# Attention and two feed-forward layers on one core: the product with v taken for two query tiles at once, and scores listed ahead of older work

## Chip, cores and metric

One core of a Trainium2 chip. The metric is the device time of one execution in microseconds (us). Engine names follow the profile: PE is TensorE (PEld its weight loads), DVE is VectorE, ACT is ScalarE, POOL is GpSimd, SP the queue that issues the DMAs.

## What is computed

Attention with a threshold, then two feed-forward layers on its output, all in float32:

```python
q, k, v: (4, 8, 576, 64)
scores = scale * q @ k.T
thresh = max(scores) - tau
scores = where(scores >= thresh, scores, -1e9)
attn = exp(scores - max(scores)); attn /= sum(attn) + 1e-9
x = (attn @ v) as (2304, 512)
h = x @ w_in1;  x = (h * sigmoid(1.702 h)) @ w_out1      # w_in (512, 2048)
h = x @ w_in2;  x = (h * tanh(softplus(h))) @ w_out2     # w_out (2048, 512)
```

## The kernel before

**Attention.** The 4 x 8 heads are worked in 16 pairs. A pair's 576 queries make four "full" tiles of 128 queries and one "mix" tile, in which the last 64 queries of both heads lie side by side; so there are 80 tiles, counted from 1 in this document. For each tile:

- `qk` (L600 is its matmul): the scores, both heads at once on the upper and lower 64 rows of PE's array, into the PSUM banks `sc`. A float32 matmul is two instructions in the profile; so a full tile's 4 matmuls are 8 instructions.
- `softmax_a`, once per head of the tile (144 times): DVE scales the scores into `ss` and takes their minimum (L622), POOL works out the threshold (L626), ACT takes the exponential into `p` (L629), DVE applies the threshold and sums (L632).
- `attend`: PE turns `p` by 128x128 transposes (L706, L701), ACT copies them from the banks `tb0` to `tb2` into `pm` and `pmt` (L717), PE multiplies with v (L731) into a quarter of the bank `tb3`, and ACT copies the result into `xo` (L738). The five chunks of keys of a full tile's product are 8 matmuls of 128 array rows by 64 columns (one per head and chunk, from `pm`) and 2 of 64 by 64 (from `pmt`), with 128 moving columns each.
- `scale_x`, once per pair: 1/sum goes through DRAM (`rt`, `r_d`, `rb`), POOL multiplies `xo` (L667) and a DMA stores it (L669).

**Weights.** A feed-forward weight arrives as float64 words. `conv_w` and `split_w` make of each 1/16 of a layer ("a weight" below) a high and a low part, by three passes on ACT (L380, L382, L400), one on POOL (L392) and four on DVE (L386, L389, L394, L402). From tile 41 on a new weight is started every 5 tiles, so 8 of the first layer's 16 weights are started inside attention. `val` goes through a ring of three buffers `sv`. The first `NWA` weights have memory of their own; those after them wait for `opened`, the end of all attention work, whose memory they take.

**Feed-forward layers.** `h1`/`o1` and `h2`/`o2`: 12 matmuls (24 for two halves) per step, L495, L540 and L911. Step h needs a weight and x; step o of a weight comes two steps later.

**Order.** Nothing is placed by hand. Every operation is listed with an engine, an estimated duration and a rank. `Order.run` plays the list through, gives each engine, whenever it is free, the ready operation of the lowest rank, and writes the program in that order; on the chip each engine then runs its own fixed sequence. A tile's scores have its number as rank, DVE's first pass 2.5 less (`SMR`), and `attend` runs two tiles behind (`AHEAD`) with the number of its own tile, products 0.1 less (`AR`). Where older transposes or products and newer scores are ready together, the older go first.

Of the kernel before, what the change touches and what calls it, by code (L numbers as in the profile page):

```python
# [21 lines left out]
DMA_RATE = 200e3  # L22
PR = 2
AR = 0.1
# [11 lines left out]
NSS = 4  # L36
NOUT = 2
NHS = 5
NWA = 12
# [161 lines left out]
def attention_then_two_ffn_kernel(  # L201
# [361 lines left out]
    nms = Ring(apool, "nm", 4, [128, 2], F32)  # L563
# [3 lines left out]
    pms = Ring(apool, "pm", NPM, [128, 512], F32)  # L567
    pmt = Ring(apool, "pmt", 2, [128, 128], F32)
# [106 lines left out]
    def attend(tl, ps, pair, rank):  # L675
# [3 lines left out]
        _, vr, _, kvr = head[b, hp]  # L679
        w = 128 if full else 64  # L680
        at = t * 128
        if t == 0:
            xo[b, hp] = xos.next()
        if full:
            plan = [(0, pms, (0, 1), 128, 512), (1, pms, (2, 3), 128, 512), (2, pmt, (4,), 128, 128)]
        else:
            plan = [(0, pms, (0, 1, 2, 3), 128, 512), (1, pmt, (4,), 64, 128)]
        where, copies, keys = {}, [], []
        for bank, ring, cs, rows, cols in plan:
            pn, kpn = ring.next()  # L690
            keys.append(kpn)
            for n, c in enumerate(cs):
                where[c] = (bank, n * 2 * w, pn)
            copies.append((bank, pn, kpn, rows, cols))

        def tr(cs):
            for c in cs:
                bank, c0, _ = where[c]
                if c == 4:
                    m = 64 * len(ps)  # L700
                    nc.tensor.transpose(tb[bank][0:m, 0:128], pair[:, 516:516 + m], ident)  # L701
                    yield
                    continue
                for i in range(len(ps)):
                    a = (P1 + 64 if i else 4) + c * 128
                    nc.tensor.transpose(  # L706
                        tb[bank][:, c0 + i * 128:c0 + (i + 1) * 128], pair[:, a:a + 128], ident)
                    yield

        for (bank, pn, kpn, rows, cols), (*_, cs, _, _) in zip(copies, plan):  # L710
            n = 1 if 4 in cs else len(ps) * len(cs)
            n = add("PE", n * 0.109 + (0.16 if bank == 0 else 0.0), lambda cs=cs: tr(cs),
                ps, [("tb", bank)], rank, steps=max(n, 2))
            if sch.fill is None and WARM:
                sch.fill = ("PE", n, 0.107, keep_warm)
            add("ACT", t_act(cols),
                lambda pn=pn, bank=bank, rows=rows, n=cols: nc.scalar.copy(pn[0:rows, 0:n], tb[bank][0:rows, 0:n]),  # L717
                [("tb", bank)], [kpn], rank)
        i = avn[0] % 2
        avn[0] += 1  # L720
        av, kav = tb[3][:, i * 128:i * 128 + w], ("tb", 3, i)

        def mm():
            for c in range(5):
                _, c0, pn = where[c]
                for i in range(2):
                    rows, at, vc = slice(0, 128), c0 + i * w, c * 128 + 64 * i
                    if c == 4:
                        rows = slice(64 * i, 64 * i + 64) if full else slice(0, 64)
                        at, vc = (0, 512) if full else (64 * i, 512 + 64 * i)  # L730
                    nc.tensor.matmul(  # L731
                        av[64 * i:64 * i + 64], vr[rows, vc:vc + 64], pn[rows, at:at + w],
# [3 lines left out]
        add("PE", len(CK) * 0.107 * (2 if full else 1) + 0.2, mm, keys + [kvr], [kav], rank - AR, steps=2 * len(CK))  # L736
        x, kx = xo[b, hp]
        add("ACT", t_act(w), lambda: nc.scalar.copy(x[:, at:at + w], av), [kav], [kx + (t,)], rank - AR)  # L738
        if not full:
            scaling.append(scale_x(b, hp))  # L740

    avn = [0]
# [32 lines left out]
    for gi, tl in enumerate(groups + [None] * AHEAD):  # L775
        first = len(sch.ops)
        if tl:
# [3 lines left out]
            if t == 0:  # L781
# [4 lines left out]
                  for i, bank in enumerate(qk(tl, gi))]  # L786
            marks.append(len(sch.ops) - 1)
            behind.append((tl, ps, pair, gi))
        if gi >= AHEAD:
            attend(*behind.pop(0))  # L790
# [208 lines left out]
```

## Time and profile before

| | |
|---|---|
| median of 3 runs | 1096.7 us (1096.17 to 1097.32) |
| the profiled execution's own time | 1097.12 us |
| its span, first to last instruction | 1095.3 us |
| busy: PE, DVE, ACT, POOL | 99%, 63%, 59%, 18% of the span |
| mean granted PE clock | 0.998 of full |
| first score of tile 1, of tile 41, of tile 80 | 5.80, 149.9, 292.1 us |
| first step of o1 | 311.9 us |

The profiled execution lies 0.4 us above the median; 1.8 us of its time lie outside the span. The last two rows cut the span in four: attention's first half, its second half, what is left of attention after the last scores (three steps of h1 are run among it), and the rest of the feed-forward layers. A busy PE in this profile is not a PE at its peak, since the ends of matmuls are modelled: what a group of matmuls costs is read from its start to the start of what follows.

### The profile page before, as it was taken

The numbers are of one execution on the slowest core, as the hardware profiler recorded it, in microseconds if no ns is written. First come the engines' busy times: TensorE is split into PE (matmuls) and PEld (weight loads), VectorE is DVE, ScalarE is ACT, GpSimd is POOL, SyncE is SP. The second block draws the span as 40 slices with busy tenths as digits, with TensorE's granted clock in tenths as the row PEclk, the third lists the DMA queues.
The fourth block names the chain that finished last, engine by engine and source line by source line (L and its number), as shares of the span: only waits on it lengthen the run. The fifth ranks groups of instructions, "written<-read, shape, count | busy, mean of one in ns | idle before, by whom it ended". The sixth has DMA issues, their size and how long they took to land.

```text
span 1095.3 us, 17534 instructions
## 1 busy us (share of the span) xinstructions
PE 1084.9 (99%) x6708; PEld 877.5 (80%) x6708; DVE 692.8 (63%) x1354; ACT 651.2 (59%) x1065; POOL 196.4 (18%) x198
## 2 busy tenths in 40 slices
PE   9999999999999999999999999999999999999998
PEld 7767776777778899888888888888888888888887
DVE  7868899999978645545522444566464555554544
ACT  5767777888856445444422444496655655655665
POOL 2323344455534303303200000000000000000000
PEclk9999999999999999999999999999999999999999
DMA  2223333444244255545510222500010010010010
GB/s 90 82 76 125 92 118 127 146 128 149 95 161 140 94 202 173 199 148 184 181 58 1 97 96 96 173 1 1 29 39 1 10 39 1 1 40 1 1 40 19
DMA packets 49156, 94.53 MB, mean 86 GB/s; under 512 B 6320, under 2 KB 24240, under 8 KB 49072
## 3 DMA queue, kind: packets, MB, share of 16 engines
q1 hardware_dynamic: 49072, 93.42, 25.7%
q8 instruction: 52, 0.85, 0.3%
q14 instruction: 32, 0.26, 0.1%
HBM read 70.78 MB, written 22.62 MB: 85 GB/s over the span
## 4 chain that ended last, share of the span: by engine, by line
PE 97%; ACT 1%; DVE 1%; issue 0%; POOL 0%; POOLq 0%; DVEq 0%; ACTq 0%
PE h L495 36%; PE tb L540 18%; PE tb L911 18%; PE tb L731 9%; PE sc L600 8%; PE tb L706 7%; PE tb L701 1%; PE tb L506 0%; DVE p L632 0%; DVE ss L622 0%; ACT p L629 0%; POOL nm L626 0%; ACT pm L717 0%; ACT xo L738 0%; ACT sv L380 0%
## 5 line engine op out<-in xcount | busy, mean ns | idle before, releaser
L873 ACT ACTIVATE ms<-ms 128x512 f32<-128x512 f32 (+1 forms) x240 | 131.4, 584 | 133.5 <-DVE ms L858 132.5
L495 PE MATMUL h<-xa,wh 128*128 128x512 f32 x640 | 197.5, 390 | 0.0
L495 PE MATMUL h<-x,wh 128*128 128x512 f32 (+1 forms) x640 | 165.2, 346 | 0.0
L495 PEld LDWEIGHTS h<-xa,wh 128*128 128x128 f32 x640 | 119.7, 188 | 24.7 <-issue 0.2
L521 ACT ACTIVATE t<-h 128x512 f32<-128x512 f32 (+1 forms) x80 | 44.5, 557 | 155.3 <-PE h L495 154.7
L632 DVE SCALAR_TENSOR_TENSOR p<-ss,nm,p 128x577 f32<-128x577 f32 x144 | 130.0, 926 | 8.1 <-ACT p L629 6.4
L629 ACT ACTIVATE p<-ss,nm 128x576 f32<-128x576 f32 x144 | 111.5, 785 | 37.9 <-DVE ss L622 37.4
L524 DVE SCALAR_TENSOR_TENSOR h<-t,h 128x512 f32<-128x512 f32 (+1 forms) x80 | 51.3, 642 | 121.4 <-ACT t L521 121.2
L883 DVE TENSOR_TENSOR ms<-ms,hs 128x512 f32<-128x512 f32 (+1 forms) x80 | 50.2, 636 | 122.3 <-ACT ms L873 122.2
L622 DVE TENSOR_SCALAR_CACHE_REDUCE ss<-sc,nqsc 128x576 f32<-128x576 f32 x144 | 112.2, 812 | 21.1 <-PE sc L600 20.4
L495 PEld LDWEIGHTS h<-x,wh 128*128 128x128 f32 x640 | 112.7, 189 | 15.8
L495 PE MATMUL h<-xa,wl 128*128 128x512 f32 x320 | 124.5, 389 | 0.0
L626 POOL TENSOR_SCALAR nm<-nm,tau_p 128x1 f32<-128x1 f32 x144 | 88.0, 612 | 168.0 <-DVE ss L622 163.6
L540 PE MATMUL tb<-gh,wh 128*128 128x512 f32 (+1 forms) x320 | 117.8, 368 | 0.0
L540 PE MATMUL tb<-gl,wh 128*128 128x512 f32 (+1 forms) x320 | 117.7, 368 | 0.0
L540 PE MATMUL tb<-gh,wl 128*128 128x512 f32 (+1 forms) x320 | 117.7, 368 | 0.0
L392 POOL TENSOR_TENSOR sv<-sv,sr 128x1024 uint32<-128x1024 uint32 x32 | 83.4, 2608 | 175.7 <-DVE sv L389 104.8
L911 PE MATMUL tb<-wh,g2h 128*128 128x512 f32 x288 | 112.1, 389 | 0.0
L911 PE MATMUL tb<-wl,g2h 128*128 128x512 f32 x288 | 112.1, 389 | 0.0
L911 PE MATMUL tb<-wh,g2l 128*128 128x512 f32 x288 | 112.0, 389 | 0.0
L495 PE MATMUL h<-x,wl 128*128 128x512 f32 (+1 forms) x320 | 110.9, 347 | 0.0
L600 PE MATMUL sc<-kq 64*128 64x288 f32 (+3 forms) x672 | 105.0, 417 | 1.0 <-DVE ss L622 0.9
(59 smaller groups left out, 1756.0 us busy)
## 6 DMA issues: line engine op xcount, KB each, us to landing
sr<-in_w_in SPq DMA_DIRECT2D x32, 512.0 KB
sr<-in_w_out SPq DMA_DIRECT2D x32, 512.0 KB
kq<-in_kq SPq DMA_DIRECT2D x16, 576.0 KB
sv<-x_d SPq DMA_DIRECT2D x16, 512.0 KB
w_d<-sv SPq DMA_DIRECT2D x16, 512.0 KB
sv<-w_d SPq DMA_DIRECT2D x16, 512.0 KB
vr<-in_v SPq DMA_DIRECT2D x16, 320.0 KB
x_d<-xo SPq DMA_DIRECT2D x16, 288.0 KB
```

Of the source, the lines that this page charges most:

```text
L392: lambda: nc.gpsimd.tensor_tensor(bits, bits, word(0), ALU.add), keys, [kval], rank, port=True)
L495: nc.tensor.matmul(hb[dst][:, 0:n], a[:, c, :], x[:, lo, c, 0:n], start=(i == 0), stop=(i == 3 * KD - 1))
L540: nc.tensor.matmul(accs[e][0][:, 0:n], a[:, es], b()[:, 0:n], start=(f == 0 and i == 0), stop=(f == KF - 1 and i == 2), skip_group_check=True,
L600: nc.tensor.matmul(dst, q, kq2[rows, k0:k0 + n], start=True, stop=True)
L622: lambda: nc.vector.tensor_scalar(n3, s3, nqsc, None, ALU.mult, ALU.min, accum_out=nm[:, 0:1]),
L626: lambda: nc.gpsimd.tensor_scalar(nm[:, 1:2], nm[:, 0:1], tau_p, 0.0, ALU.add, ALU.add),
L629: lambda: nc.scalar.activation(p[:, at:at + S], ns[:, 4:4 + S], AF.Exp, bias=nm[:, 0:1], scale=-1.0),
L632: lambda: nc.vector.scalar_tensor_tensor(p[:, whole], ns[:, 3 + i:4 + S + i], nm[:, 1:2], p[:, whole], ALU.is_le, ALU.mult, accum_out=sums ...
L706: nc.tensor.transpose(tb[bank][:, c0 + i * 128:c0 + (i + 1) * 128], pair[:, a:a + 128], ident)
L731: nc.tensor.matmul(av[64 * i:64 * i + 64], vr[rows, vc:vc + 64], pn[rows, at:at + w], start=(c == 0), stop=(c == 4))
L873: nc.scalar.activation(m()[:, 0:n], m()[:, 0:n], fn, bias=bias)
L911: nc.tensor.matmul(accs[t][0], x[:, t * 128:(t + 1) * 128], w, start=(f == 0 and i == 0), stop=(f == KF - 1 and i == 2), skip_group_check= ...
```

## The change

`attend` is split into `turn` and `product`. `turn` transposes one tile as before, but the copies of two neighbouring full tiles go into the same `pm` and `pmt` buffers, which are twice as wide, 128 columns of each tile in turn; the copies' destination is thus in pieces of 128 columns. After every second full tile (and after each mix tile) `product` is listed: the same 10 matmuls as for one tile, now with 256 moving columns, into half of `tb3`, followed by one copy of 256 columns to `xo`. It is no longer one operation of the list but three (chunks 0-1, 2-3, 4), each of which needs only its own copies, so other PE work may come between them; a key "product" keeps all products in sequence. Scores are ranked 8 tiles (`SF`) lower, so they go before any older transposes and products. `ss` has 6 buffers for 4, `nm` 8 for 4, and to make room the weights with memory of their own fall from 12 to 9. What is computed is the same.

```diff
--- before.py
+++ after.py
@@ -20,6 +20,7 @@
 SMR = 2.5
 DMA_US = 2.0
 DMA_RATE = 200e3
+SF = 8
 PR = 2
 AR = 0.1
 NORM_P = 1.0
@@ -33,10 +34,10 @@
 SLACK = 0.0
 AHEAD = 2
 NP = 8
-NSS = 4
+NSS = 6
 NOUT = 2
 NHS = 5
-NWA = 12
+NWA = 9
 NPM = 4
 NKQ = 2
 NXO = 2
@@ -560,12 +561,12 @@
     vrs = Ring(apool, "vr", NKQ, [128, 5 * 128], F32)
     pps = Ring(apool, "p", NP // 2, [128, P1 + S + 1], F32)
     sss = Ring(apool, "ss", NSS, [128, S + 5], F32)
-    nms = Ring(apool, "nm", 4, [128, 2], F32)
+    nms = Ring(apool, "nm", 8, [128, 2], F32)
     sms = Ring(apool, "sm", 2, [128, 32], F32)
     rts = Ring(apool, "rt", 1, [128, 32], F32)
     rbs = Ring(apool, "rb", 1, [128, S], F32)
-    pms = Ring(apool, "pm", NPM, [128, 512], F32)
-    pmt = Ring(apool, "pmt", 2, [128, 128], F32)
+    pms = Ring(apool, "pm", NPM, [128, 1024], F32)
+    pmt = Ring(apool, "pmt", 2, [128, 256], F32)
     xos = Ring(apool, "xo", NXO, [128, S], F32)
     xo = {}
     sm = {}
@@ -672,73 +673,89 @@
 
         return [multiply, spread, invert]
 
-    def attend(tl, ps, pair, rank):
+    def turn(tl, ps, pair, rank):
 
         kind, b, hp, t = tl
         full = kind == "full"
-        _, vr, _, kvr = head[b, hp]
-        w = 128 if full else 64
-        at = t * 128
         if t == 0:
             xo[b, hp] = xos.next()
         if full:
-            plan = [(0, pms, (0, 1), 128, 512), (1, pms, (2, 3), 128, 512), (2, pmt, (4,), 128, 128)]
+            if t % 2 == 0:
+                turned[b, hp] = [pms.next(), pms.next(), pmt.next()]
+            plan = [(0, (0, 1), 128), (1, (2, 3), 128), (2, (4,), 128)]
         else:
-            plan = [(0, pms, (0, 1, 2, 3), 128, 512), (1, pmt, (4,), 64, 128)]
-        where, copies, keys = {}, [], []
-        for bank, ring, cs, rows, cols in plan:
-            pn, kpn = ring.next()
-            keys.append(kpn)
+            turned[b, hp] = [pms.next(), pmt.next()]
+            plan = [(0, (0, 1, 2, 3), 128), (1, (4,), 64)]
+
+        def tr(bank, cs):
             for n, c in enumerate(cs):
-                where[c] = (bank, n * 2 * w, pn)
-            copies.append((bank, pn, kpn, rows, cols))
-
-        def tr(cs):
-            for c in cs:
-                bank, c0, _ = where[c]
                 if c == 4:
                     m = 64 * len(ps)
                     nc.tensor.transpose(tb[bank][0:m, 0:128], pair[:, 516:516 + m], ident)
                     yield
                     continue
                 for i in range(len(ps)):
-                    a = (P1 + 64 if i else 4) + c * 128
-                    nc.tensor.transpose(
-                        tb[bank][:, c0 + i * 128:c0 + (i + 1) * 128], pair[:, a:a + 128], ident)
+                    a, c0 = (P1 + 64 if i else 4) + c * 128, (n * len(ps) + i) * 128
+                    nc.tensor.transpose(tb[bank][:, c0:c0 + 128], pair[:, a:a + 128], ident)
                     yield
 
-        for (bank, pn, kpn, rows, cols), (*_, cs, _, _) in zip(copies, plan):
+        for (bank, cs, rows), (pn, kpn) in zip(plan, turned[b, hp]):
             n = 1 if 4 in cs else len(ps) * len(cs)
-            n = add("PE", n * 0.109 + (0.16 if bank == 0 else 0.0), lambda cs=cs: tr(cs),
+            cols = 128 * n
+            n = add("PE", n * 0.109 + (0.16 if bank == 0 else 0.0), lambda bank=bank, cs=cs: tr(bank, cs),
                 ps, [("tb", bank)], rank, steps=max(n, 2))
             if sch.fill is None and WARM:
                 sch.fill = ("PE", n, 0.107, keep_warm)
-            add("ACT", t_act(cols),
-                lambda pn=pn, bank=bank, rows=rows, n=cols: nc.scalar.copy(pn[0:rows, 0:n], tb[bank][0:rows, 0:n]),
-                [("tb", bank)], [kpn], rank)
+            src = tb[bank][0:rows, 0:cols]
+            dst = pn[0:rows, 0:cols]
+            if full:
+                dst = pn[0:rows].rearrange("p (g q) -> p g q", q=256)[:, :, t % 2 * 128:t % 2 * 128 + 128]
+                src = src.rearrange("p (g q) -> p g q", q=128)
+            add("ACT", t_act(cols), lambda src=src, dst=dst: nc.scalar.copy(dst, src),
+                [("tb", bank)], [kpn + (t % 2,)], rank)
+        if not full or t % 2:
+            product(tl, rank)
+
+    def product(tl, rank):
+
+        kind, b, hp, t = tl
+        full = kind == "full"
+        _, vr, _, kvr = head[b, hp]
+        w = 256 if full else 64
+        at = t // 2 * 256
+        pn = [p for p, _ in turned[b, hp]]
+        parts = ((0, 1), (2, 3), (4,)) if full else ((0, 1, 2, 3), (4,))
         i = avn[0] % 2
         avn[0] += 1
-        av, kav = tb[3][:, i * 128:i * 128 + w], ("tb", 3, i)
-
-        def mm():
-            for c in range(5):
-                _, c0, pn = where[c]
+        av, kav = tb[3][:, i * 256:i * 256 + w], ("tb", 3, i)
+
+        def mm(cs):
+            for c in cs:
                 for i in range(2):
-                    rows, at, vc = slice(0, 128), c0 + i * w, c * 128 + 64 * i
-                    if c == 4:
-                        rows = slice(64 * i, 64 * i + 64) if full else slice(0, 64)
-                        at, vc = (0, 512) if full else (64 * i, 512 + 64 * i)
+                    rows, vc = slice(0, 128), c * 128 + 64 * i
+                    if c < 4 and full:
+                        p, a = pn[c // 2], (c % 2 * 2 + i) * 256
+                    elif c < 4:
+                        p, a = pn[0], c * 128 + i * 64
+                    elif full:
+                        rows, p, a, vc = slice(64 * i, 64 * i + 64), pn[2], 0, 512
+                    else:
+                        rows, p, a = slice(0, 64), pn[1], 64 * i
                     nc.tensor.matmul(
-                        av[64 * i:64 * i + 64], vr[rows, vc:vc + 64], pn[rows, at:at + w],
+                        av[64 * i:64 * i + 64], vr[rows, vc:vc + 64], p[rows, a:a + w],
                         start=(c == 0), stop=(c == 4))
                     yield
 
-        add("PE", len(CK) * 0.107 * (2 if full else 1) + 0.2, mm, keys + [kvr], [kav], rank - AR, steps=2 * len(CK))
+        for cs, (_, kp) in zip(parts, turned[b, hp]):
+            add("PE", len(cs) * (0.49 if full else 0.13) + 0.05, lambda cs=cs: mm(cs),
+                [kp + (h,) for h in range(2 if full else 1)] + [kvr], [kav, "product"], rank - AR, steps=2 * len(cs))
         x, kx = xo[b, hp]
-        add("ACT", t_act(w), lambda: nc.scalar.copy(x[:, at:at + w], av), [kav], [kx + (t,)], rank - AR)
+        add("ACT", t_act(w), lambda: nc.scalar.copy(x[:, at:at + w], av), [kav],
+            [kx + (j,) for j in ((t - 1, t) if full else (t,))], rank - AR)
         if not full:
             scaling.append(scale_x(b, hp))
 
+    turned = {}
     avn = [0]
     scaling = []
 
@@ -783,11 +800,11 @@
             sums, ksum = sm[b, hp]
             pair, kpair = pps.next()
             ps = [softmax_a(sums, ksum, 5 * i + t, gi, bank, (pair, kpair), i)
-                  for i, bank in enumerate(qk(tl, gi))]
+                  for i, bank in enumerate(qk(tl, gi - SF))]
             marks.append(len(sch.ops) - 1)
             behind.append((tl, ps, pair, gi))
         if gi >= AHEAD:
-            attend(*behind.pop(0))
+            turn(*behind.pop(0))
             for todo in list(scaling):
                 todo.pop()(gi - AR, [marks[min(gi, len(marks) - 1)]] if tl else [])
                 if not todo:
```

How this moves instructions is seen in the programs' order (L706, L701, L731 of before are L699, L694, L744 of the change; L600 and L400 are one line further down). `tb0` to `tb3`, `sc`, `p`, `pm` and `pmt` are the tiles named above, with buffer numbers; "x4" means four equal matmuls in a row.

First place, on PE: what stands ahead of the first scores of pair 4 (tile 16). Before, the last 11 of the 19 rows between the scores of tile 15 and these:

```order
L731 MATMUL tb3_94<-pm2_174,vr0_154 64x128 x4
L731 MATMUL tb3_94<-pm3_175,vr0_154 64x128 x4
L731 MATMUL tb3_94<-pmt0_176,vr0_154 64x128 x2
L701 MATMUL tb2_93<-ident_100,p1_157 128x128
L706 MATMUL tb0_91<-ident_100,p2_158 128x128 x4
L701 MATMUL tb1_92<-ident_100,p2_158 64x128
L731 MATMUL tb3_94<-pm0_172,vr0_154 64x128 x4
L731 MATMUL tb3_94<-pm1_173,vr0_154 64x128 x4
L731 MATMUL tb3_94<-pmt1_177,vr0_154 64x128 x2
L731 MATMUL tb3_94<-pm2_174,vr0_154 64x64 x8
L731 MATMUL tb3_94<-pmt0_176,vr0_154 64x64 x2
L600 MATMUL sc0_98<-kq1_153 128x288
```

And now, all rows between the same two scores, and what follows:

```order
L699 MATMUL tb1_92<-ident_100,p2_152 128x128 x4
L699 MATMUL tb0_91<-ident_100,p3_153 128x128 x4
L694 MATMUL tb2_93<-ident_100,p3_153 128x128
L699 MATMUL tb1_92<-ident_100,p3_153 128x128 x4
L601 MATMUL sc0_98<-kq1_147 128x288
L601 MATMUL sc1_99<-kq1_147 128x288
L601 MATMUL sc0_98<-kq1_147 128x288
L601 MATMUL sc1_99<-kq1_147 128x288
L744 MATMUL tb3_94<-pm2_174,vr0_148 64x256 x4
```

Before, everything left of the older tiles, four tiles' products among it, stood ahead of these scores; now four rows of transposes do, and a product's first parts follow the scores.

Second place, on PE: around the scores of tile 54, in pair 11. Before, what stands between the scores of tiles 54 and 55:

```order
L731 MATMUL tb3_94<-pm2_174,vr0_154 64x128 x4
L731 MATMUL tb3_94<-pm3_175,vr0_154 64x128 x4
L731 MATMUL tb3_94<-pmt0_176,vr0_154 64x128 x2
L706 MATMUL tb0_91<-ident_100,p3_159 128x128 x4
L706 MATMUL tb1_92<-ident_100,p3_159 128x128 x4
L701 MATMUL tb2_93<-ident_100,p3_159 128x128
L600 MATMUL sc0_98<-kq0_152 64x288
```

And now:

```order
L744 MATMUL tb3_94<-pm1_173,vr1_149 64x256 x4
L699 MATMUL tb1_92<-ident_100,p2_152 128x128 x4
L699 MATMUL tb0_91<-ident_100,p3_153 128x128 x4
L694 MATMUL tb2_93<-ident_100,p3_153 128x128
L601 MATMUL sc0_98<-kq0_146 128x288
L601 MATMUL sc1_99<-kq0_146 128x288
L601 MATMUL sc0_98<-kq0_146 128x288
L601 MATMUL sc1_99<-kq0_146 128x288
L744 MATMUL tb3_94<-pm2_174,vr1_149 64x256 x4
L744 MATMUL tb3_94<-pmt1_177,vr1_149 64x256 x2
L699 MATMUL tb1_92<-ident_100,p3_153 128x128 x4
L699 MATMUL tb0_91<-ident_100,p0_150 128x128 x4
```

A product was one piece of ten matmuls for one tile; now its three parts (pm1, pm2, pmt1) serve two tiles, and transposes and scores stand between the first part and the other two.

Third place, on ACT: the first layer's weights around the end of attention. `t` and `gh` are made by each step of h1 from its bank `h`, `wh` is the high part of a weight. Before, around weight 9 (weights are counted from 0):

```order
L526 CAST gh2_147<-h1_3114 128x512
L400 CAST wh9_134<-sv2_115 128x1024
L521 ACTIVATE t0_143<-h2_3115 128x512
L380 ACTIVATE sv1_114<-sr2_112 128x1024
L382 ACTIVATE sr2_112<-sr2_112 128x1024
L526 CAST gh0_145<-h2_3115 128x512
L521 ACTIVATE t1_144<-h3_3116 128x512
L400 CAST wh10_136<-sv0_113 128x1024
```

And now:

```order
L522 ACTIVATE t1_138<-h1_2736 128x512
L527 CAST gh2_141<-h1_2736 128x512
L401 CAST wh9_3055<-sv2_115 128x1024
L401 CAST wh10_3057<-sv0_113 128x1024
L401 CAST wh11_3059<-sv1_114 128x1024
L381 ACTIVATE sv2_115<-sr0_110 128x1024
L522 ACTIVATE t0_137<-h2_2737 128x512
```

The high parts of weights 9, 10 and 11 waited for nothing but their own data; now they stand in one piece, need the memory of attention, and the `t` of a later step stands behind them.

## Rows read from the trace of the kernel before

**Rows 1.** Windows: stretch, us, busy of PE, PEld, DVE, ACT, POOL, PE's clock, DMA.

```profile
149.90:292.10 142.20, 141.10 (x1426) 101.07 (x1425) 137.21 (x316) 117.52 (x237) 71.33 (x84) 1.00 0.42 137
5.80:149.90 144.10, 141.81 (x1407) 101.86 (x1406) 121.16 (x303) 101.17 (x216) 48.16 (x78) 0.99 0.28 86
```

**Rows 2.** The chain that ended last, in order of time: start, us, what.

```profile
311.94 2.94 PE tb L540 x12
314.88 2.72 PE h L495 x12
...
1080.55 10.92 PE tb L911 x48
```

**Rows 3.** Timeline of PE, 199 to 204: start, us, array rows*columns, shape, instructions.

```profile
199.69 1.09 PE L731 MATMUL tb<-pm,vr 128*64 128x128 f32 x16
200.71 0.44 PE L731 MATMUL tb<-pmt,vr 64*64 64x128 f32 x4
201.08 1.09 PE L706 MATMUL tb<-ident,p 128*128 128x128 f32 x8
...
202.21 1.20 PE L600 MATMUL sc<-kq 64*64 64x288 f32 x10
203.34 0.66 PE L706 MATMUL tb<-ident,p 128*128 128x128 f32 x4
```

**Rows 4.** Timeline of PE, 286 to 290; the first three are a mix tile's.

```profile
286.44 0.69 PE L731 MATMUL tb<-pm,vr 128*64 128x64 f32 x16 [0.33 <-ACT pm L717]
287.06 0.33 PE L731 MATMUL tb<-pmt,vr 64*64 64x64 f32 x4
287.32 1.09 PE L706 MATMUL tb<-ident,p 128*128 128x128 f32 x8
...
288.45 1.24 PE L600 MATMUL sc<-kq 64*128 64x288 f32 x8
289.62 1.09 PE L731 MATMUL tb<-pm,vr 128*64 128x128 f32 x16
```

**Rows 5.** Timeline, 62 to 67; in brackets the idle time before, and its end.

```profile
62.03 1.24 PE L600 MATMUL sc<-kq 64*128 64x288 f32 x8
63.30 0.82 DVE L622 TENSOR_SCALAR_CACHE_REDUCE ss<-sc,nqsc 128x576 f32<-128x576 f32 x1 [5.63 <-PE sc L600]
64.18 1.97 PE L600 MATMUL sc<-kq 64*128 64x288 f32 x8 [0.91 <-DVE ss L622]
66.85 1.51 PE L706 MATMUL tb<-ident,p 128*128 128x128 f32 x7 [0.44 <-DVE p L632]
```

**Rows 6.** Windows, the stretch behind it.

```profile
67.20:70.50 3.30, 3.30 (x15) 2.15 (x13) 1.90 (x6) 2.58 (x5) 1.20 (x2) 0.50 0.01 2
```

**Rows 7.** Groups by line and shape: busy us, mean ns of one, idle before.

```profile
L402 DVE TENSOR_TENSOR wl<-sv,wh 128x1024 fp32r<-128x1024 f32 x32 | 40.0, 1251 | 16.1 <-ACT wh L400 16.1
L394 DVE SCALAR_TENSOR_TENSOR sv<-sr,sv 128x1024 uint32<-128x1024 uint32 x32 | 38.8, 1216 | 9.5 <-POOL sv L392 9.4
L382 ACT ACTIVATE sr<-sr 128x1024 f32<-128x1024 uint32 x32 | 37.3, 1169 | 0.0
L400 ACT CAST wh<-sv 128x1024 fp32r<-128x1024 f32 x32 | 33.8, 1056 | 14.4 <-PE tb L540 8.4 <-DVE sv L394 5.9
L386 DVE TENSOR_SCALAR sv<-sv 128x1024 f32<-128x1024 f32 x32 | 28.1, 879 | 5.0 <-ACT sv L380 5.0
L389 DVE TENSOR_SCALAR sv<-sv 128x1024 uint32<-128x1024 uint32 x32 | 25.9, 809 | 0.3
```

**Rows 8.** Timeline of attention's end, 308 to 331.

```profile
309.14 0.66 PE L706 MATMUL tb<-ident,p 128*128 128x128 f32 x4 [0.73 <-DVE p L632]
310.99 0.69 PE L731 MATMUL tb<-pm,vr 128*64 128x64 f32 x16 [1.09 <-ACT pm L717]
...
330.08 0.59 ACT L526 CAST gh<-h 128x512 fp32r<-128x512 f32 x1
330.25 0.33 SPq L669 DMA_DIRECT2D x_d<-xo  x1
```

## The prediction

> **What bounds the kernel now.** I read the chain of waits first, in order of time. From 311.9 us on it is PE alone: 12 matmuls every 2.72 us to the last group at 1080.6 [rows 2]. Nothing in the diff touches these steps, so their 783 us stay, and the change can only move the moment at which the first step of o1 starts.
>
> Then windows over attention, cut where the scores of tile 41 and of tile 80 start. In both halves PE is busy nearly throughout, but DVE differs: 121.2 of 144.1 us in the first half, 137.2 of 142.2 in the second, where the weights are prepared beside attention [rows 1]. So the first half is PE's, and the second belongs to PE and DVE together.
>
> A busy PE says little here, so I read PE's timeline from start to start. A full tile's product takes 1.39 us (199.69 to 201.08), nine transposes 1.13 (to 202.21), a mix tile's scores 1.13 [rows 3]; a full tile's scores take 1.17 (288.45 to 289.62), a mix tile's product 0.88 (286.44 to 287.32) [rows 4]. The reader is to see one more thing there, the price of changing the array's shape (rows*columns in the timeline; I call a stretch of one shape a run). 16 instructions of 128 columns cost 1.02 us, 16 of 64 columns 0.62: 64 columns are worth 0.40, so 128 stream for 0.80 and 0.22 is the run's own. For the four 64*64 ones it is 0.37 against 0.26, so 0.15 is the run's own [rows 3, 4]. Transposes have a run of 0.16 if each takes 0.108.
>
> Last, where PE loses time. Ahead of pair 4's scores stand four tiles' older work. DVE runs dry for 5.63 us, then PE waits 0.91 and 0.44 for DVE [rows 5], and right behind it, from 67.2 to 70.5, the granted clock is 0.50, which is 1.2 GHz where the rest has 2.4 [rows 6].
>
> **The change, part by part.**
>
> *Wider products.* Half as many product instructions of twice the columns stream as long. What falls is runs. Counted over PE's order up to the last product: 345 changes of shape before, 290 now. In one piece each the wider products would save two runs per pair of tiles, 64; their cutting into parts gives some back, and other neighbours join. 55 x 0.16 = 8.8 us less PE work. The bounds: if a run costs more the longer its instructions are (the 8 of 288 columns: 1.17 less 0.91 of streaming at the above rate leaves 0.26), some 80 long product runs cost 0.1 each more than I count, and 1 us is left; at 0.22 for all it is 12.
>
> *Scores first.* The same counts, up to the first score of tile 41: 163 changes of shape before, 129 now; 314 transposes before, 288 now; products of 30 full and 7 mix tiles before, 28 and 6 now. A full product streams for 0.80 + 0.22 = 1.02 us, a mix one for half of it. So 34 x 0.16 = 5.4, 26 x 0.108 = 2.8, and 2 x 1.02 + 0.5 = 2.5 of streaming lie no longer ahead of these scores: 10.7 us. The crowding before pair 4 goes too (four rows of transposes are left there): its two waits, 1.35, and half of 3.3 us at half the clock, 1.65, make 3.0. First half: -13.7.
>
> In the second half PE's work falls by 26 runs, 7 transposes and one product: 4.2 + 0.8 + 1.0 = 6.0. But DVE must follow. Its order now has one weight more between these scores (7, 7, 6 and 5 of the four passes, for 6, 6, 5 and 4): 0.88 + 0.81 + 1.22 + 1.25 = 4.2 us [rows 7], and one L632 of 0.8 less. 137.2 + 4.2 - 0.8 = 140.6 of the 142.2 it had. Second half: -1.6, DVE full.
>
> What was put off comes after the last scores: 56 transposes for 23, products of 6 full and 2 mix tiles for 3 and 1, 18 changes of shape for 13: 3.6 + 3.6 + 0.8 = 8.0 us more PE work. The rest of attention took 19.8 us (292.1 to 311.9), with 0.73 and 1.09 of waits at its end [rows 8]. These go: DVE has five threshold passes and one weight left after the last scores, about 9 us, and PE some 24 us of other work before it needs the last of them. Rest: +6.2.
>
> Sum: -13.7 - 1.6 + 6.2 = -9.1.
>
> *Copies.* The copies to `pm` write four pieces of 128 columns. No row shows that form. From below it costs nothing; from above I take the nearest strided destination, L382 at 1169 ns against the plain L400 at 1056, 11% [rows 7]. Even if all of ACT's 117.5 us in the second half grew by 11%, 13 us, its 24.7 idle us cover it [rows 1]. I take zero. 32 fewer copies to `xo` come off an engine that isn't the bound: zero.
>
> *Buffers.* Two more `ss` and four more `nm` take no time. Fewer own weights: weights 9 to 11 wait for attention's memory, thus for the last store. It was issued 18.3 us after o1's start, 21.1 after the last threshold pass let PE go on (309.1 to 330.25) [rows 8]. Now the last threshold pass comes about 16 us ahead of o1's start (9 after the last scores, of 26), so the store is issued about 5 us after it. On ACT the high parts of weights 9 to 11 stand behind the `gh` of step 5, which ran 18.2 us after o1's start [rows 8]. Covered by 13 us: zero.
>
> *Queues.* The DMAs are the same. The loads of v wait for products that come later, and the next pair's k and q stand behind them on SP; five tiles of scores, some 17 us, lie between. Zero.
>
> **A rule against these numbers.** By rows, a matmul's fixed cost is at most 0.22/16 = 14 ns, if the whole of a run's own cost is put on its instructions; 640 fewer instructions then save 9.0 us, as the runs do [rows 4]. The Trainium skill, page "TensorEngine Tiling (Array Packing)", section on instruction overhead, gives each matmul about 60 cycles, and one column the latency of sixty. At 2.4 GHz that is 25 ns, an estimate from that page, and 640 instructions would save 16 us; the sum would be -16.3.
>
> **Rivals.**
>
> *PE alone is the bound* (0.22). If weights slide or DVE's passes wait less for POOL, the second half gains its 6.0 and some of what PE lost there. -13.7 - 6.0 + 6.2 = -13.5: 1083.6, down to 1080. For it: PE is busy 141.1 of 142.2 us there. Against: DVE is full too.
>
> *DVE swallows the head start* (0.14). Scores can be early only as far as DVE takes them from two `sc` tiles. If the first half wins its 10.7 without the waits, the second nothing, and the rest still pays 6.2, it is -4.5: 1092.6. For it: DVE 96% busy in the second half. Against: the first half has 23 us of idle DVE.
>
> *A cost per matmul, not per run* (0.04). At 25 ns each, 7.2 us more than the 8.8: 1080.8. Against: 16 half-length instructions take 0.62 us; streaming 0.40 and 16 x 25 ns make 0.80. The page named above gives this price.
>
> *The late weights stall* (0.04), the slower case. If the last store lands later than 23 us after o1's start, the three casts on ACT (3 us), `t`, `gh` and `gl` of step 6 and the three DVE passes behind them, some 9 us in all, no longer fit before o1's step 6, at 6 x 2 x 2.72 = 32.6; each us later costs one, so the whole is slower than before from 32 on, some 27 later than worked out. Landed at 37 it costs 14: 1102. Against: that needs a chain of 21 us to become more than twice as long.
>
> *Clock or order gone wrong* (0.04). Each stretch like that at 67.2 costs 1.65. It came after PE had waited; six of them eat the gain, and more make it slower: 1099.
>
> The forecast has 0.52.
>
> **How the numbers follow.** The profiled execution took 1097.1 us, 0.4 above the median. 1097.1 - 9.1 = 1088.0. The likeliest case alone reaches from 1085 to 1091. The range, 1080 to 1093.5, takes in PE alone and DVE's swallowing; what is left out is part of the two ends, under 2 in 10. A change under 0.2%, 2.2 us, can't be told from none here. Faster: 0.52 + 0.22 + 0.04 and most of 0.14, less a little for what I have not seen, 0.86; same 0.06; slower 0.08.
>
> **What would show it.** Right: the first score of tile 41 at about 136 us for 149.9, of tile 80 at about 277 for 292.1, o1's first step near 303 for 311.9, and steps of 2.72 us from there on. A two-tile product in one piece takes 2 x 1.02 of streaming and runs of 0.22 and 0.15 from start to start, 2.4 us against 2 x 1.39. No 5 us of idle DVE before pair 4, and no halved clock there. Wrong: score starts no earlier at tile 41 (the order's counts are not what PE is bound by); tile 80 as early as 272 (PE alone); waits of PE for `ss` in the second half over 8 us (DVE swallows); a gap in the steps after o1's start, ended by a cast of weights 9 to 11 (late weights).

## The result, and the profile after

The change made the kernel slower: 1112.7 us median (1109.5 to 1113.5, 4 runs) for 1096.97, a ratio of 1.0134 with an interval of 1.0121 to 1.0148. 1088.0 was forecast, so both the sign and the range were missed. The profiled execution took 1113.5 us, its span 1111.7.

First the windows that answer to [rows 1], cut where the scores of tile 41 and of tile 80 and the first step of o1 start, and two short stretches that answer to [rows 6]. The columns are start and end, length, then busy time of PE, PEld, DVE, ACT and POOL, the granted clock, DMA.

```profile
core 0: us, PE busy (x) PEld busy (x) DVE busy (x) ACT busy (x) POOL busy (x), PEclk, DMA share, GB/s
5.80:143.80 138.00, 133.31 (x1041) 83.37 (x1040) 115.46 (x297) 93.83 (x189) 40.99 (x77) 1.00 0.29 91
143.80:297.30 153.50, 141.22 (x1100) 87.85 (x1100) 141.31 (x317) 113.42 (x217) 69.25 (x84) 0.97 0.39 122
297.30:328.30 31.00, 25.69 (x203) 18.42 (x203) 25.62 (x38) 23.45 (x44) 11.24 (x7) 1.00 0.44 145
195.10:198.40 3.30, 3.30 (x17) 1.71 (x15) 2.50 (x8) 0.77 (x2) 1.02 (x2) 0.50 0.24 64
222.40:229.20 6.80, 6.50 (x40) 4.18 (x40) 4.66 (x11) 3.16 (x8) 1.01 (x2) 0.50 0.14 38
```

The first half took 138.0 us for 144.1, 6.1 less (13.7 was forecast). The second took 153.5 for 142.2, 11.3 more (1.6 less), and the rest of attention 31.0 for 19.8, 11.2 more (6.2). Here is the chain of waits where attention ends, beside [rows 2].

```profile
322.36 0.48 ACT pm L714
...
325.46 0.37 ACT xo L753
325.83 0.22 ACT sr L383
...
326.78 0.59 ACT pm L714
...
327.41 0.95 PE tb L744 x20
328.36 2.96 PE tb L541 x12
331.32 2.72 PE h L496 x12
```

From o1's first step on nothing changed: steps of 2.72 us, and 1111.7 - 328.3 = 783.4 us to the end, as before. The loss lies ahead of it, and the reader sees the new link of the chain: ACT's copy to `pm`, and the work ahead of that copy on ACT.

PE is no longer busy throughout: in the second half 12.3 of 153.5 us are idle, where [rows 1] had 1.1 of 142.2. What it waited for in attention, in us, times and the longest, first in the kernel before:

```profile
PE tb L706 <- DVE p L632: 1.5, 3, 0.7
PE tb L731 <- ACT pm L717: 1.4, 2, 1.1
PE tb L731 <- ACT xo L738: 1.1, 3, 0.4
PE sc L600 <- DVE ss L622: 0.9, 1, 0.9
```

and in the changed kernel:

```profile
PE tb L744 <- ACT pm L714: 10.1, 15, 1.7
PE sc L601 <- DVE ss L623: 7.2, 7, 2.2
PE tb L699 <- ACT pm L714: 1.7, 4, 0.6
PE tb L744 <- ACT xo L753: 1.4, 3, 0.5
```

4.9 us have become 20.4: products wait for their copies, and scores for DVE. With idle stretches too short for this list (under 0.15 us), PE was idle for 5.2 us of attention before and for 22.3 now, as the windows have it. Waits can also hide in time that the view counts as busy. Read from start to start, as the prediction reads costs, with all that a run of one shape takes beyond its own cost counted as a wait, the two traces give some 13 and 38 us, by an estimate from all of PE's runs; the 13 and 37 us named in the expectations below are to be read against these.

How a product comes to wait shows in two timelines of the changed kernel. Of PE (start, length, instruction, in brackets the idle time ahead and what ended it):

```profile
300.30 1.95 PE L744 MATMUL tb<-pm,vr 128*64 128x256 f32 x16 [0.58 <-ACT pm L714]
302.17 0.65 PE L744 MATMUL tb<-pmt,vr 64*64 64x256 f32 x4
302.75 0.66 PE L699 MATMUL tb<-ident,p 128*128 128x128 f32 x4
303.25 0.38 PE L694 MATMUL tb<-ident,p 128*64 128x128 f32 x2
305.31 0.69 PE L744 MATMUL tb<-pm,vr 128*64 128x64 f32 x16 [1.68 <-ACT pm L714]
...
322.89 1.95 PE L744 MATMUL tb<-pm,vr 128*64 128x256 f32 x16 [1.74 <-ACT pm L714]
...
327.41 0.69 PE L744 MATMUL tb<-pm,vr 128*64 128x64 f32 x16 [1.30 <-ACT pm L714]
```

and of ACT ahead of the wait of 1.68 us:

```profile
300.77 2.79 ACT L630 ACTIVATE p<-ss,nm 128x576 f32<-128x576 f32 x4
303.45 0.38 ACT L753 COPY xo<-tb 128x256 f32<-128x256 f32 x1
303.70 1.07 ACT L401 CAST wh<-sv 128x1024 fp32r<-128x1024 f32 x1
304.65 0.61 ACT L714 COPY pm<-tb 128x512 f32<-128x512 f32 x1
```

The four transposes of the mix tile that this product needs first are done at about 303.4. Their copy stands on ACT behind four exponentials, a copy to `xo` and a weight cast, and starts 1.2 us later, at 304.65; the product stands next in PE's queue, so PE waits 1.68 us.

### The profile page after: what moved, and what is told of

Read it like the earlier page. It is cut to its first block, busy times and chain, and to the rows that moved or that the text cites. A ratio compares the mean times of both kernels' runs of the same rounds, so it can differ in the third digit from the quotient of the medians.

```text
span 1111.7 us, 16158 instructions
## 1 busy us (share of the span) xinstructions
PE 1084.3 (98%) x6068; PEld 850.6 (77%) x6068; DVE 692.3 (62%) x1358; ACT 646.5 (58%) x1033; POOL 182.4 (16%) x198
## 4 chain that ended last, share of the span: by engine, by line
PE 90%; ACT 5%; DVE 3%; issue 1%; DMA 1%; SPq 0%; POOL 0%; DVEq 0%; ACTq 0%; POOLq 0%
PE h L496 35%; PE tb L541 18%; PE tb L928 18%; PE sc L601 7%; PE tb L744 7%; PE tb L699 4%; ACT pm L714 2%; ACT p L630 1%; DVE p L633 1%; DVE ss L623 1%; PE tb L694 0%; PE tb L507 0%; ACT pmt L714 0%; DMA vr<-in_v 0%; ACT sr L383 0%
## 5 line engine op out<-in xcount | busy, mean ns | idle before, releaser
L633 DVE SCALAR_TENSOR_TENSOR p<-ss,nm,p 128x577 f32<-128x577 f32 x144 | 134.2, 953 | 25.9 <-ACT p L630 13.2
L630 ACT ACTIVATE p<-ss,nm 128x576 f32<-128x576 f32 x144 | 108.7, 790 | 17.2 <-DVE ss L623 17.1
L601 PE MATMUL sc<-kq 64*128 64x288 f32 (+3 forms) x672 | 107.4, 421 | 7.3 <-DVE ss L623 7.2
L393 POOL TENSOR_TENSOR sv<-sv,sr 128x1024 uint32<-128x1024 uint32 x32 | 80.7, 2523 | 187.0 <-DVE sv L390 133.2
L627 POOL TENSOR_SCALAR nm<-nm,tau_p 128x1 f32<-128x1 f32 x144 | 76.9, 534 | 183.3 <-DVE ss L623 177.6
```

Of the source, the lines that this page charges most:

```text
L393: lambda: nc.gpsimd.tensor_tensor(bits, bits, word(0), ALU.add), keys, [kval], rank, port=True)
L601: nc.tensor.matmul(dst, q, kq2[rows, k0:k0 + n], start=True, stop=True)
L627: lambda: nc.gpsimd.tensor_scalar(nm[:, 1:2], nm[:, 0:1], tau_p, 0.0, ALU.add, ALU.add),
L630: lambda: nc.scalar.activation(p[:, at:at + S], ns[:, 4:4 + S], AF.Exp, bias=nm[:, 0:1], scale=-1.0),
L633: lambda: nc.vector.scalar_tensor_tensor(p[:, whole], ns[:, 3 + i:4 + S + i], nm[:, 1:2], p[:, whole], ALU.is_le, ALU.mult, accum_out=sums ...
```

## Experiments

Each table row is one kernel: its time, its ratio to the kernel before with the interval, then the idle time of PE just ahead of products, scores and transposes in attention by the trace's groups of instructions, and the changes of array shape up to the last product, counted as in the prediction.

| kernel | us | ratio | products | scores | transposes | changes |
|---|---|---|---|---|---|---|
| before | 1096.97 | 1 | 2.7 | 1.0 | 1.5 | 345 |
| changed | 1112.7 | 1.0134 [1.0121, 1.0148] | 12.0 | 7.3 | 3.0 | 290 |
| e1 wide product, old order | 1121.8 | 1.0227 [1.0206, 1.0247] | 7.0 | 17.1 | 2.6 | 269 |
| e2 scores first, old product | 1089.0 | 0.9932 [0.9917, 0.9947] | 0.2 | 1.4 | 0.8 | 359 |
| e3 buffers alone | 1095.9 | 0.9996 [0.9986, 1.0005] | 1.7 | 1.5 | 1.8 | 343 |
| e4 changed, SF = 2 | 1105.4 | 1.0072 [1.0053, 1.0091] | 9.5 | 5.5 | 1.8 | 286 |
| e5 paired, 128 columns | 1096.25 | 0.9997 [0.9988, 1.0007] | 0.0 | 4.1 | 3.6 | 312 |
| e6 changed, products put off | 1092.8 | 0.9959 [0.9947, 0.9971] | 0.5 | 5.4 | 1.5 | 274 |
| e7 products put off, SF = 4 | 1081.2 | 0.9859 [0.9842, 0.9876] | 0.5 | 2.9 | 0.3 | 265 |
| e8 changed, SF = 4 | 1094.9 | 0.9979 [0.9970, 0.9989] | 9.0 | 3.3 | 2.1 | 285 |
| e9 changed, five pairs of p | 1103.3 | 1.0065 [1.0050, 1.0080] | 9.7 | 3.3 | 2.8 | 299 |
| e10 changed, 4 ss | 1097.7 | 1.0012 [1.0002, 1.0021] | 5.2 | 1.4 | 7.1 | 273 |
| e11 changed, no GpSimd pass | 1100.6 | 1.0037 [1.0023, 1.0052] | 10.8 | 1.7 | 2.9 | 290 |
| e12 e7, product in one piece | 1092.9 | 0.9972 [0.9959, 0.9985] | 2.1 | 3.4 | 4.4 | 243 |
| e13 e8, no GpSimd pass | 1090.9 | 0.9950 [0.9935, 0.9964] | 8.8 | 2.6 | 1.4 | 285 |
| e14 e7, 128 columns | 1091.3 | 0.9953 [0.9938, 0.9968] | 0.5 | 0.9 | 2.2 | 324 |
| e15 e6, 4 ss | 1088.4 | 0.9925 [0.9911, 0.9940] | 0.5 | 3.2 | 2.0 | 270 |
| e16 e7, 4 ss | 1082.2 | 0.9872 [0.9855, 0.9888] | 0.9 | 2.8 | 0.7 | 267 |

**Which part of the change it is.** e1 is the wide product alone:

```diff
-SF = 8
+SF = 0
```

> The widened product alone: scores keep the rank of their own tile (SF = 0), all else as in the changed kernel. PE's order up to the last product has 269 changes of array shape, for 345 before and 290 with the whole change. Theory A (putting the scores first is what makes PE wait): the waits of PE in attention fall back to the 13 us of before, and 76 x 0.16 = 12 us of work are gone: about 1084.5 us. Theory B (the widened product makes PE wait, since it needs the copies of two tiles and leaves less other work between a copy and its use): the 37 us of waits stay, and 1112.7 less 21 x 0.16 is about 1109 us.

e2 is the scores first alone, e3 the buffers alone, both on the kernel before; e4 is the changed kernel with `SF = 2`.

```diff
+SF = 4
-NSS = 4
+NSS = 6
-NWA = 12
+NWA = 9
-    nms = Ring(apool, "nm", 4, [128, 2], F32)
+    nms = Ring(apool, "nm", 8, [128, 2], F32)
-                  for i, bank in enumerate(qk(tl, gi))]
+                  for i, bank in enumerate(qk(tl, gi - SF))]
```

> The scores first alone, with the product of one tile at 128 columns as before, and the change's buffers (6 ss, 8 nm, 9 own weights). The scores are ranked 4 tiles ahead, not 8: PE's order is then the same row for row as with 8. 359 changes of shape for 345: 2.2 us more work. Theory A: the waits of PE come as in the changed kernel, 37 for 13 us: about 1097 + 2 + 24 = 1123 us. Theory B: the waits stay near 13 us: 1097 to 1101 us.

> The kernel before with the change's buffers alone: 6 ss for 4, 8 nm for 4, 9 own weights for 12; 343 changes of shape for 345. Theories A and B both: no difference that can be told, 1095 to 1098 us. Theory C (the fewer own weights or the deeper rings cost): slower, up to 1112 us if they are the whole loss.

> The changed kernel with the scores ranked 2 tiles ahead instead of 8, so that they tie with the older tiles' work instead of passing all of it. 286 changes of shape for 290. Theory A: the waits go with the rank, so between 1085 and 1100 us. Theory B: the waits stay, about 1111 us.

Theory A fell: scores first alone is a gain of 8 us, where neither theory expected a gain, and the wide product alone costs 25. The buffers are nothing. So the loss came with the wide product (theory B), more of it than B expected in e1, where PE waits 17.1 us ahead of scores. e4 lies between what the two theories expected, so how far ahead the scores stand matters too. Counted over e1's trace, 45 of 74 stretches from one tile's scores to the next hold no full tile's product (17 of 74 before).

**What about the wide product it is.** e5 holds the product back to every second tile, but computes it tile by tile, with `SF = 4`; e6 changes one number; e7 has `SF = 4` beside it, e8 `SF = 4` alone. The edit of e6,

```diff
-                [kp + (h,) for h in range(2 if full else 1)] + [kvr], [kav, "product"], rank - AR, steps=2 * len(cs))
+                [kp + (h,) for h in range(2 if full else 1)] + [kvr], [kav, "product"], rank + 1.1, steps=2 * len(cs))
```

and of e5, where `o` is the column at which a tile starts:

```diff
-        for cs, (_, kp) in zip(parts, turned[b, hp]):
-            add("PE", len(cs) * (0.49 if full else 0.13) + 0.05, lambda cs=cs: mm(cs),
-                [kp + (h,) for h in range(2 if full else 1)] + [kvr], [kav, "product"], rank - AR, steps=2 * len(cs))
+        for o in (0, 128) if full else (0,):
+            for cs, (_, kp) in zip(parts, turned[b, hp]):
+                add("PE", len(cs) * (0.245 if full else 0.13) + 0.05, lambda cs=cs, o=o: mm(cs, o),
+                    [k + (h,) for _, k in turned[b, hp] for h in range(2 if full else 1)] + [kvr],
+                    [kav, "product"], rank - AR, steps=2 * len(cs))
```

> The product of two tiles is still listed in one go behind the copies of the second tile, but computed tile by tile with 128 moving columns, as before; scores ranked 4 tiles ahead, as in e2. So this is e2 with its products held back to every second tile, and nothing is wider. 312 changes of shape for e2's 359: 7.5 us less work than e2. Theory B1 (holding a product back to every second tile is the loss: between two tiles' scores PE then has only 1.1 us of transposes, while DVE needs two passes of 0.74 us and the way there and back before the next scores can be written): about 1089 - 7.5 + 24 = 1105 us, 1100 to 1115. Theory B4 (the wide instructions themselves or the wide buffers cost): 1081 to 1089 us.

> The changed kernel with one number changed: the three parts of a two-tile product are ranked 1.1 tiles later than their tile (rank + 1.1 for rank - 0.1), so that transposes go first and the parts are left to stand between scores. Copies, buffers, widths and the scores' rank stay. 274 changes of shape for 290: 2.6 us less work. Theory B1: the waits of PE fall from 37 to 10 to 15 us: about 1112.7 - 2.6 - 24 = 1086 us, 1080 to 1092. Theory B2 (PE waits because its copies stand behind exponentials on ACT, whatever the order of the products): at most a third of the waits goes, 1100 to 1110 us. Theory B4: 1108 to 1112 us.

> As e6, with the scores ranked 4 tiles ahead. 265 changes of shape: 4.0 us less work than the changed kernel, 12.8 less than before. Theory B1: waits of 8 to 13 us, 1078 to 1086 us, and less than e2's 1089.0, since e2 has 94 x 0.16 = 15 us more work of shapes. Theory B2: 1098 to 1108 us. Theory B4: 1107 to 1111 us.

> The changed kernel with the scores ranked 4 tiles ahead and nothing else: the base for e7, and beside e2 and e5 the wide, paired case at the same rank of the scores. 285 changes of shape for 290. All theories: within 5 us of the changed kernel's 1112.7.

e6 and e7 decide it. The same wide product, copies and buffers, with the products listed a tile later, are 19.9 us (e6 against the changed kernel) and 13.7 us (e7 against e8) faster, and the products' waits fall from 12.0 and 9.0 us to 0.5. e5 bears it out from the other side: it has 7.5 us less work than e2, by the price of 0.16 us a shape, and is 7.3 us slower, so holding products back cost about 15 us without any wide instruction. That is less than the 24 expected, and e6 missed its range by 0.8. e8 broke what all theories expected of it: 17.8 us between 8 and 4 tiles ahead. A stretch of PE in e7:

```profile
196.65 1.09 PE L699 MATMUL tb<-ident,p 128*128 128x128 f32 x8
197.58 0.27 PE L694 MATMUL tb<-ident,p 128*128 128x128 f32 x1
197.78 1.24 PE L601 MATMUL sc<-kq 64*128 64x288 f32 x8
198.96 0.66 PE L699 MATMUL tb<-ident,p 128*128 128x128 f32 x4
199.45 0.27 PE L694 MATMUL tb<-ident,p 128*64 128x128 f32 x1
199.65 1.95 PE L744 MATMUL tb<-pm,vr 128*64 128x256 f32 x16
201.53 1.24 PE L601 MATMUL sc<-kq 64*128 64x288 f32 x8
202.70 0.65 PE L744 MATMUL tb<-pmt,vr 64*64 64x256 f32 x4
```

Between the transposes of 196.65 and their product at 199.65 lie 1.2 us of scores and 0.7 us of other transposes, and two of the product's parts frame the next scores. Whatever ACT has ahead of the copies is covered; the row of waits for `pm` is gone from this kernel:

```profile
PE sc L601 <- DVE ss L623: 2.8, 3, 1.4
PE tb L744 <- ACT xo L753: 0.5, 1, 0.5
```

e12 keeps the late rank, but lists the product in one piece:

```diff
-        for cs, (_, kp) in zip(parts, turned[b, hp]):
...
+        add("PE", 5 * (0.49 if full else 0.13) + 0.15, lambda: mm(range(5)),
+            [kp + (h,) for _, kp in turned[b, hp] for h in range(2 if full else 1)] + [kvr], [kav, "product"],
+            rank + 1.1, steps=10)
```

> As e7 (products ranked 1.1 tiles later, scores 4 tiles ahead), but a tile pair's product is one piece instead of three, and waits for all its copies. 243 changes of shape for e7's 265: 3.5 us less work. Theory B1 (PE needs pieces of product between two tiles' scores, so cutting and putting off belong together): the waits come back in the gaps without a product, 8 to 18 us: 1086 to 1096 us. If the cutting doesn't matter: 1077 to 1080 us.

It is 11.7 us slower than e7 with 3.5 us less work: cutting into parts and putting them off belong together.

**Why 8 tiles ahead is worse than 4.** In the changed kernel the scores of 5 or 6 more tiles have started when a tile's transposes begin (55 of 70 tiles), in e8 2 or 3, in e7 3. e9 gives `p` a fifth pair, e10 takes `ss` back to 4, e11 leaves the GpSimd pass over the weights out: it runs on one column of 1024, so this kernel's weights lack what the pass adds.

```diff
-NP = 8
-NWA = 9
+NP = 10
+NWA = 8
```

```diff
-NSS = 6
+NSS = 4
```

```diff
-            lambda: nc.vector.tensor_scalar(bits, bits, 3, None, ALU.logical_shift_left),
+            lambda: nc.vector.tensor_scalar(bits, bits, 0, None, ALU.logical_shift_left),
-            lambda: nc.gpsimd.tensor_tensor(bits, bits, word(0), ALU.add), keys, [kval], rank, port=True)
+            lambda: nc.gpsimd.tensor_tensor(bits[:, 0:1], word(0)[:, 0:1], word(0)[:, 0:1], ALU.subtract), keys, [kval], rank, port=True)
```

> The changed kernel (scores 8 tiles ahead, products not put off) with five pairs of p instead of four and 8 own weights instead of 9 to make room. In the changed kernel the scores start 5 or 6 tiles ahead of the transposes of their tile, which is more than four pairs of p hold; in the kernel with 4 tiles ahead (1094.9) they lead by 2 or 3. Theory S (the scores run ahead until p and ss are full, and then each stage waits for the one behind it): with a fifth pair the waits shrink, 1095 to 1106 us. Theory Q (scores listed that early wait in PE's queue for DVE whatever the depth, with ready work behind them): 1108 to 1116 us.

> The changed kernel with 4 ss buffers, as before, instead of 6. Theory S: the lead falls, since a tile's first pass on DVE needs an ss that the thresholds have freed, and the time goes the way of the kernel with 4 tiles ahead: 1095 to 1106 us. Theory Q: 1108 to 1116 us. If the shorter ring itself costs: over 1116 us.

> The changed kernel without the GpSimd pass over the weights: the add runs on one column of 1024, and the shift ahead of it is by 0, so the weights lose their low part. PE's order is the same row for row. Theory P (the loss of the second half is set off by the GpSimd pass: a threshold pass of DVE beside it takes 2.6 to 3.0 us instead of 0.8, the scores wait 1.6 to 2.2 us, and the clock is halved behind such a wait): three such waits, 6 us, and 5 us of halved clock go: 1099 to 1105 us. Theories B1 and S: the waits for copies stay, 1107 to 1112 us.

e13 is e11's edit with `SF = 4`; e15 and e16 are e10's on e6 and e7.

> The kernel with scores 4 tiles ahead (1094.9) without the GpSimd pass over the weights, left out as in e11. Theory S (it is the lead of 5 to 6 tiles that makes that pass costly, since then the scores wait for DVE with nothing between): little is won here, 1091 to 1095 us. Theory P alone (the pass costs PE the same wherever the scores stand): as much less as in e11, some 8 us beside the clock's share: 1084 to 1088 us.

> e6 (products put off, scores 8 tiles ahead, 1092.8) with 4 ss instead of 6, so that the scores can't run as far ahead. Theory S: 1081 to 1086 us, as with 4 tiles ahead. Theory Q (the rank itself): 1090 to 1094 us.

> e7 with 4 ss instead of 6; 267 changes of shape for 265. The lead is 3 tiles in e7 already, so Theory S expects no difference: 1080 to 1083 us. If the two more buffers are what lets DVE go on beside its slow passes: 1084 to 1090 us.

e9, e10 and e11 all win: 9.4, 15.0 and 12.1 us. The GpSimd pass sets off the two longest waits for scores, as the trace of the changed kernel shows for one of them on DVE, POOL and PE:

```profile
190.36 2.79 DVE L633 SCALAR_TENSOR_TENSOR p<-ss,nm,p 128x577 f32<-128x577 f32 x1 [0.37 <-ACT p L630]
...
193.08 0.81 DVE L633 SCALAR_TENSOR_TENSOR p<-ss,nm,p 128x577 f32<-128x577 f32 x1
...
193.82 0.81 DVE L623 TENSOR_SCALAR_CACHE_REDUCE ss<-sc,nqsc 128x576 f32<-128x576 f32 x1
```

```profile
190.13 2.40 POOL L393 TENSOR_TENSOR sv<-sv,sr 128x1024 uint32<-128x1024 uint32 x1 [1.41 <-ACT pmt L714]
```

```profile
194.69 1.86 PE L601 MATMUL sc<-kq 64*64 64x288 f32 x10 [2.18 <-DVE ss L623]
```

A threshold pass that starts beside the GpSimd pass takes 2.79 us for 0.81, the scores' pass behind it comes late, PE's next entry is scores, and PE waits 2.18 us; then the clock is halved for 3.4 us (the window at 195.1). The second stretch, at 222.4, follows a wait of 1.90 us of the same kind. In e8 and e7 DVE has such long passes too, but no halved clock. e13 says that the pass alone costs 4.0 us when the scores lead by 2 or 3, against 12.1 when they lead by 5 or 6 (3.4 of these are the clock: 10.2 us at half of it against 3.4). So the pass costs more where the scores stand further ahead, which is against theory P alone.

The pass is not all of it. Without it, 8 tiles ahead is still 9.7 us slower than 4 (e11 and e13), where the table has 2.6 us more of idle time and 0.8 us more of shapes. Nor does the lead by itself put the kernels in order (theory S): with a fifth pair it grows, to 6 in 38 of 70 tiles, and e9 still won; and it is 3 or 4 in e6 already, in 69 of 70 tiles, as in e15, where 4 `ss` change it little and yet win 4.4 us. What differs there is the clock: attention runs three stretches at half clock in e6's trace,

```profile
169.70:173.10 3.40, 3.40 (x16) 1.74 (x17) 2.52 (x8) 2.08 (x4) 1.01 (x2) 0.50 0.00 0
227.70:231.10 3.40, 3.40 (x18) 1.44 (x14) 2.11 (x7) 1.23 (x2) 1.13 (x3) 0.51 0.25 41
282.40:285.80 3.40, 3.40 (x18) 1.83 (x17) 2.11 (x5) 2.00 (x4) 3.40 (x4) 0.50 0.43 127
```

which cost 5.1 us, half of their length, and none in e15's. e15 came out between S and Q, and why it stays 7.2 us above e7 is open: 0.8 us are shapes and 2.0 are waits that the table shows (5.7 for 3.7), 4.4 have no row. So what 8 tiles ahead cost beside the pass and the clock isn't shown.

**What the width is worth.** e14 is e7 with the product computed tile by tile at 128 columns, by e5's loop over `o`, each part behind its own copies.

> e7 with the pair's product computed tile by tile at 128 moving columns, each in three parts: what the width itself is worth once the waits are gone. 324 changes of shape for e7's 265. If a run costs 0.16 us, as the prediction priced it: 59 x 0.16 = 9.4 us more than e7, 1089 to 1092 us. If a run is worth little and the width nothing: 1081 to 1084 us. If each of the 640 more instructions costs 25 ns: 1096 to 1099 us.

It costs 10.1 us more, with the same waits (3.6 us in the table for 3.7). Put on the 59 changes of shape that is 0.17 us each, where the prediction had 0.16. e14 has 640 more instructions as well, and by itself can't tell the two apart: put on these it is 16 ns each. e7's trace can:

```profile
192.87 1.08 PE L744 MATMUL tb<-pm,vr 128*64 128x256 f32 x8
193.89 1.24 PE L601 MATMUL sc<-kq 64*128 64x288 f32 x8
```

From start to start 8 instructions of 256 columns take 1.02 us, and 16 of 128, the same columns, took 1.02 too [rows 3]. 16 ns each would make 0.13 us of difference. So the price is mostly that of the change of shape. The rule of the Trainium skill, page "TensorEngine Tiling (Array Packing)", section on instruction overhead, would by estimate have made it 16 us for the instructions alone; the measurement decides against it here.

## Why the prediction was wrong, step by step

- **Wider products, -8.8: right.** A two-tile product took 2.45 us in one piece (300.30 to 302.75; forecast 2.4), and e14 with e7's trace confirms the price of a run.
- **Copies, costed at zero: the step that failed.** Their form costs nothing, as said: 591 ns on average, 588 before. But "its 24.7 idle us cover it" set the sum of ACT's idle time against the sum of the copies' cost. Idle time in sum covers nothing for a copy that stands last in 3.9 us of ACT's work without a gap (300.77 to 304.65) when the product is PE's next entry. The prediction's sum has no term for such a hand-over. What should have been costed is the PE work that the order leaves between a tile's copies and its product; the products' waits went from 2.7 to 12.0 us.
- **Scores first, first half -13.7: measured -6.1.** The counts of the work were of the order that was run; the waits were taken as given, less those before pair 4. Those went (no stretch at half clock there), and others came. e2 has this part by itself: its scores of tile 41 start at 142.1 us, 7.8 earlier, and it gains 8.0 us in all, though it has 2.2 us more of shapes and the forecast's -9.1 holds 8.8 for the wider products. In e7, where most of the waits are gone, the scores of tiles 41 and 80 start at 137.6 and 274.9 us, near the 136 and 277 forecast.
- **Second half -1.6, "DVE full": +11.3.** DVE was busy 141.3 of 153.5 us, near the 140.6 forecast, so its work was right and its fullness wasn't the bound. PE waited for copies, and for DVE, longest where the GpSimd pass held it.
- **Rest of attention +6.2: +11.2.** The 5 us between are the waits of 0.58, 1.68, 1.74 and 1.30 us for copies that PE's timeline shows there, 5.3 in all.
- **Buffers, queues: right.** e3 is the same as before, and o1's steps stay as they were; no late weight.
- **The sum.** -8.8 of work, +17.1 of idle time (5.2 to 22.3), +3.4 for the clock (10.2 us at half of it for 3.4, half of the difference) make 11.7 of the 16.4 us that attention grew. 4.7 us have no row. By the estimate from start to start, about 10 us of work went, 25 us of waits came and 3 of clock, which leaves under 2; so most of the 4.7 are waits in time that the view counts as busy.
- **The rivals.** The nearest was "clock or order gone wrong" (0.04, 1099 us). It put its price on the clock, which cost 3.4 us; the order's waits cost 17.1 in idle time alone. "DVE swallows" named a sign, waits for `ss` above 8 us in the second half, that was nearly met (7.2 in all), yet they were the smaller part.

e7 beats both kernels: 1081.2 us, a ratio of 0.9859, with the wide products, their parts listed 1.1 tiles later, and the scores 4 tiles ahead.

## What to carry over

When a change pulls two pieces of work into one, ask what the in-order queue of the busy engine now has between a producer and its consumer: idle time of another engine, as a sum, covers no single hand-over. Cut the merged piece and list its parts late, as filler between the pieces that wait for other engines. Listing work further ahead doesn't pay without end: scores 4 tiles ahead beat 8 here by 17.8 us, and by 11.6 with the products put off. Only a part of that has its cause shown.

## What the hardware showed

The granted clock fell to half, 1.2 GHz, in stretches of 3.4 and 6.8 us; in the changed kernel they came 0.4 and 1.0 us after PE had gone on from waits of 2.18 and 1.90 us. In e7, whose longest wait was 1.4 us, attention has none. The length of the wait doesn't decide it by itself: in e6 the clock fell 2.1 and 1.9 us after waits of 1.31 and 1.35 us (PE went on at 167.63 and 280.48), in e12 right after one of 0.98 us (248.26) and not after one of 2.14 us (304.1), and in e5 not after one of 1.79 us (292.04).

DVE's threshold pass took 2.79 us beside a GpSimd pass over the weights and 0.81 without: it ends 0.62 us after GpSimd's end (193.15 and 192.53), so most of its own 0.81 us came after that. The Trainium skill, page "SBUF — State Buffer", section "SBUF: two separate sides", calls the port pair of the two an exclusive lock that the later one waits out; the trace agrees. With the GpSimd pass left out, e11's threshold passes averaged 861 ns for 953.
